# Attention with a hand-laid TensorE order: score matmuls spread over a head's slot, norm steps spread over slots

**The chip, the cores and the metric.** One core of a Trainium2 chip. The metric is device time in microseconds (us). Every kernel was run four to seven times, the kernel before again in each round; medians are quoted, with lowest and highest. Ratios are the mean time of one kernel's fast runs over the mean of the kernel before in the same rounds, so they are not quite the ratio of the quoted medians; in brackets stands the 95% interval. The experiments ran on two chips (6 and 9 to 12 on one, the others on another), so compare them by ratios. Every run here was of the fast state. A trace shows one run of each kernel; where that was not a typical one, the text says so.

## The reference

```python
def reference(A_x, A_k_cache, A_v_cache, A_wq, A_wo, B_x, B_w1, B_w2, B_w3, B_w4):
    x = A_x                                  # 1 x 2048 x 576
    xn = _layernorm(x, axis=-1)
    s = _A_ref(xn, ...)   # 32 heads of 128 dims over the last 512 keys of 16 kv heads, then @ wo
    g = _silu(_B_ref(xn, ...))
    # B: h = gelu(LN(xn) @ w1); four channel groups shifted along the sequence; x1 = xn + shifted @ w2
    #    out = x1 + gelu(LN(x1) @ w3) @ w4          (F = 4608)
    return x + s * g
```

## The kernel before

The sequence is cut into four blocks of 512 rows. Attention walks through 128 *slots*, one per head and block. A slot holds the next head's q (5 matmuls of 512 columns), this head's scores (4 of 512), the last head's value product (16 of 129), and now and then a *filler*: the output projection (wo) of the block before, W1 or W2. The MLP with w3 and w4 follows.

```python
        ps_sc = pool("ps_sc", 3, PSUM)       # score banks
        ps_pq = pool("ps_pq", 2, PSUM)       # q and W1
        ps_po = pool("ps_po", 2, PSUM)       # value product
        ps_wo = pool("ps_wo", 1, PSUM)
        ...                                  # cut
        def stage_s(u):
            ...
            for kc in range(KCH):            # four score matmuls, one after the other
                sc = ps_sc.tile([P, QB], FP32, name="sc", tag="sc")
                nc.tensor.matmul(sc[:, :], lhsT=kT[:, g, kc * P:(kc + 1) * P], rhs=qT[:, :], start=True, stop=True)
                pT = pT_pool.tile([P, QB], BF16, name="pT")
                nc.scalar.activation(out=pT[:, :], in_=sc[:, :], func=ACT.Exp, scale=SCALE)
        ...                                  # cut
            at(base + 8, lambda b=b: ln2(b))                    # norm before W1
            for tt in range(TB):
                at(base + 9, lambda b=b, tt=tt: tr2(b, tt))     # its transposes, sync engine's queue
        ...                                  # cut
        for j in range(2, NB * 8):
            at(4 * (j - 1), lambda j=j: load_wq(j))             # wq for four heads, two buffers
        ...                                  # cut
        with tc.manual_schedule(engines={SP, POOL}):            # TensorE is left to the scheduler
            for u in range(0, max(U + 2, last) + 1):
                if u + 1 < U:
                    stage_q(u + 1)
                if u < U:
                    stage_s(u)
                if 0 <= u - 1 < U:
                    stage_v(u - 1)
                if 0 <= u - 2 < U:
                    stage_t(u - 2)
                for fn in fill.get(u, []):
                    fn()
```

Loads of wq, v and x1 and the DMA transposes (o to oT per head, the normed block to xnnT for W1 and to xT for the next q, kT) all stand in the sync engine's queue, in the order of these slots. GpSimd's queue loads W1, W2, wo and x.

Names in the lines below: `sc` are scores, `pT` their exps, `po` the value product (`o` once it is scaled), `psq` is q before its copy to `qT`, `ph` and `psx` are the results of W1 and W2, `pswo` that of wo, `hs` is a part of W1's output that is copied with a shift for W2, and `x1` is W2's result, which is stored and loaded again for the MLP's norm. VectorE also takes maxima of wq and kT; a flag made of them tells whether the scores are small enough for an exp without a maximum taken off.

## Time and profile before

| | before |
|---|---|
| median of 4 runs (908.18 to 909.05) | 908.82 us |
| span in the profile, mean granted clock | 905.1 us, 0.988 |
| TensorE busy | 95% |
| bare slot, block 0 / blocks 1 to 3 | 3.06 / 3.10 us |
| slot with a W1 filler, blocks 1 to 3 | 4.17 us |
| slot with a wo filler | 10.00 us |
| time of one block (first exp to first exp of the next), blocks 0, 1, 2 | 111.8, 141.8, 142.3 us |

Slot times are distances between the first exps of successive heads. A *stop*, here and below, is the distance between the starts of two matmuls in a row less the columns of the first at 2.4 per ns, worked out from the trace. It is a little longer than the same wait in a list of waits, which counts from a modelled end. The lines behind this are in the prediction. The four timed runs of before are not the profiled one, which took 906.96 us.

### The profile page before, as it was taken

Reading aid. Unit: us, or ns where it says so; the run is one execution under the profiler, and the core shown is the slowest. Engines: PE = TensorE matmul, PEld = TensorE weight load, DVE = VectorE, ACT = ScalarE, POOL = GpSimd, SP = SyncE. Lnnn points to the kernel's source line nnn. Section 1 sums busy time; section 2 is a strip of 40 time slices with the busy share of each in tenths; the row PEclk is TensorE's granted clock in tenths of the full one; section 3 lists DMA queues with packets and bytes.
Section 4 is the critical chain, followed back from the end, with each engine's and each line's share of the span. In section 5 each row is a group of like instructions: output and inputs, shape, how many; then the busy total and the mean of one; then the engine's idle time right before and its main releaser. Section 6 shows DMA issues by size and latency. Waiting matters only on the chain.

```text
span 905.1 us, 15932 instructions
## 1 busy us (share of the span) xinstructions
PE 859.1 (95%) x6304; PEld 473.4 (52%) x6412; DVE 394.4 (44%) x1237; ACT 433.6 (48%) x814; POOL 36.9 (4%) x75
## 2 busy tenths in 40 slices
PE   5999799999999999999998998999999999999996
PEld 2655465555565465555564554554444444444454
DVE  7689653469882337652126644300026008005023
ACT  2666473277784366686345666122233223224510
POOL 1503000000000100000000000100000000000000
PEclk9999899999999999999999999999999999999998
DMA  5998931162543243362134245695005003101001
GB/s 125 183 211 191 212 95 48 30 149 62 112 101 81 34 112 88 91 121 62 39 84 104 56 114 111 169 342 138 1 7 154 1 1 132 30 1 53 1 14 43
DMA packets 165073, 83.73 MB, mean 93 GB/s; under 512 B 120064, under 2 KB 163328, under 8 KB 164992
## 3 DMA queue, kind: packets, MB, share of 16 engines
q1 hardware_dynamic: 158944, 71.57, 33.9%
q0 software_dynamic: 2640, 7.83, 3.8%
q10 hardware_dynamic: 3408, 3.25, 1.1%
q8 instruction: 52, 0.85, 0.4%
q14 instruction: 29, 0.24, 0.1%
HBM read 47.07 MB, written 9.44 MB: 62 GB/s over the span
## 4 chain that ended last, share of the span: by engine, by line


## 5 line engine op out<-in xcount | busy, mean ns | idle before, releaser
L306 ACT ACTIVATE pT<-sc 128x512 bf16<-128x512 f32 x512 | 266.0, 608 | 48.2 <-PE sc L304 48.1
L319 PEld LDWEIGHTS <-pT 128*128 128x128 bf16 x2048 | 141.4, 99 | 76.5 <-issue 16.5
L564 PE MATMUL ph<-xT_b,w_s 128*128 128x512 bf16 x701 | 171.0, 380 | 0.9
L319 PE MATMUL po<-v_sb,pT 128*128 128x129 bf16 x2048 | 164.2, 222 | 7.1 <-DVE o L323 7.0
L289 PE MATMUL psq<-xT_b,wq_b 128*128 128x512 bf16 x600 | 154.2, 384 | 8.1 <-DMA wq_b<-in_A_wq_dram 6.0
L304 PE MATMUL sc<-qT,kT 128*128 128x512 bf16 x512 | 154.9, 384 | 6.1
L567 ACT ACTIVATE h<-ph 128x512 bf16<-128x512 f32 x144 | 85.7, 596 | 155.5 <-PE ph L564 150.2
L573 PE MATMUL pm<-w_s,h 128*128 128x512 bf16 x523 | 143.4, 380 | 0.1
L322 DVE RECIPROCAL ri<-po 128x2 f32<-128x2 f32 x256 | 42.7, 167 | 184.3 <-PE po L319 182.9
L584 DVE TENSOR_TENSOR bs<-pm,x 128x512 f32<-128x512 f32 (+3 forms) x18 | 11.1, 633 | 251.5 <-PE pm L573 203.6
L347 PE MATMUL pswo<-wo_sb,oT 128*128 128x512 bf16 x497 | 111.3, 380 | 1.0 <-issue 0.2
L323 DVE TENSOR_TENSOR o<-po,ri 128x256 bf16<-128x256 f32 x256 | 108.0, 422 | 6.4 <-DVE ri L322 0.3
L564 PEld LDWEIGHTS <-w_s 128*128 128x128 bf16 x720 | 63.8, 98 | 73.4
L574 PE MATMUL pr<-w_s,h 128*128 128x64 bf16 x540 | 99.2, 193 | 0.8
L295 ACT ACTIVATE qT<-psq 128x512 bf16<-128x512 f32 x96 | 57.3, 597 | 80.4 <-PE psq L289 80.3
L289 PEld LDWEIGHTS <-wq_b 128*128 128x128 bf16 x640 | 59.4, 98 | 64.7 <-DMA wq_b<-in_A_wq_dram 6.9
L573 PEld LDWEIGHTS <-h 128*128 128x128 bf16 x540 | 52.6, 98 | 63.7 <-issue 0.6
L347 PEld LDWEIGHTS <-oT 128*128 128x128 bf16 x512 | 49.6, 98 | 57.0
L304 PEld LDWEIGHTS <-kT 128*128 128x128 bf16 x512 | 50.6, 99 | 45.9 <-issue 1.8
L350 ACT ACTIVATE s_out<-pswo 128x512 bf16<-128x512 f32 x16 | 9.6, 597 | 104.2 <-PE pswo L347 104.2
L574 PEld LDWEIGHTS <-h 128*128 128x128 bf16 x540 | 51.1, 98 | 12.2 <-issue 0.4
L586 ACT ACTIVATE th<-bs 128x576 f32<-128x576 f32 (+3 forms) x18 | 11.0, 626 | 44.5 <-DVE bs L584 44.5
(85 smaller groups left out, 455.7 us busy)
## 6 DMA issues: line engine op xcount, KB each, us to landing
wq_b<-in_A_wq_dram SPq DMA_DIRECT2D x32, 512.0 KB, 4.0
w_s<-in_B_w_dram SPq DMA_DIRECT2D x9, 576.0 KB, 8.1
wo_sb<-in_A_wo_dram POOLq DMA_DIRECT2D x4, 1152.0 KB, 7.7
w_s<-in_B_w_dram SPq DMA_DIRECT2D x9, 512.0 KB, 9.0
x_dram<-x SPq DMA_DIRECT2D x4, 576.0 KB, 3.5
x<-x_dram SPq DMA_DIRECT2D x4, 576.0 KB, 4.4
s_b<-s_dram SPq DMA_DIRECT2D x4, 576.0 KB, 6.0
x_b<-in_A_x_dram SPq DMA_DIRECT2D x4, 576.0 KB, 5.6
```

The costliest lines, as they stand in the source:

```text
L289: nc.tensor.matmul(psq[:, :], lhsT=w[:, kc, hh * Dh:(hh + 1) * Dh], rhs=xT_b[qb % 2][:, kc, :], start=(kc == 0), stop=(kc == NDC - 1))
L295: nc.scalar.activation(out=qT[:, :], in_=psq[:, :], func=ACT.Copy)
L304: nc.tensor.matmul(sc[:, :], lhsT=kT[:, g, kc * P:(kc + 1) * P], rhs=qT[:, :], start=True, stop=True)
L306: nc.scalar.activation(out=pT[:, :], in_=sc[:, :], func=ACT.Exp, scale=SCALE)
L319: nc.tensor.matmul(po[:, j, :], lhsT=pTs[kc][:, tt * P:(tt + 1) * P], rhs=v_sb[:, g, kc, 0:Dh + 1], start=(kc == 0), stop=(kc == KCH - 1))
L322: nc.vector.reciprocal(out=ri[:], in_=po[:, :, Dh])
L323: nc.vector.tensor_tensor(out=o[:, t0:t0 + 2, :], in0=po[:, :, 0:Dh], in1=ri[:].unsqueeze(2).to_broadcast([P, 2, Dh]), op=ALU.mult)
L347: nc.tensor.matmul(st["ps"][:, :], lhsT=oT_t[qb * Hq + h][:, tt, :], rhs=wo_sb[:, h, 0:M0], start=(h == 0), stop=(h == Hq - 1))
L564: nc.tensor.matmul(ph[:, :], lhsT=w3[:, kc, f0:f0 + P], rhs=xT_b[b % 2][:, kc, :], start=(kc == 0), stop=(kc == NDC - 1))
L567: nc.scalar.activation(out=h3[:, :], in_=ph[:, :], func=ACT.Gelu_apprx_tanh)
L573: nc.tensor.matmul(pm[tt][:, :], lhsT=lhsT, rhs=w4[:, fc % WS, 0:M0], start=(fc == 0), stop=(fc == FC - 1))
L574: nc.tensor.matmul(pr[:, tt, :], lhsT=lhsT, rhs=w4[:, fc % WS, M0:D], start=(fc == 0 and tt == 0), stop=(fc == FC - 1), skip_group_check=True)
```

## The change

Its intent: no burst of scores, hence no wait for a score bank; and no long run of norm operations on VectorE (DVE). The core of the diff:

```diff
-        with tc.manual_schedule(engines={SP, POOL}):
+        with tc.manual_schedule(engines={SP, POOL, PE}):
 ...
+                atoms = pe_fill.get(u, [])
+                cut = [atoms[0:n // 3], atoms[n // 3:2 * n // 3], atoms[2 * n // 3:]]
+                for i in range(4):
+                    if u < U:
+                        stage_s(u, i)
+                    if i == 0:
+                        if u + 1 < U:
+                            stage_q(u + 1)
+                        for fn in fill.get(u, []):
+                            fn()
+                        continue
+                    if i < 3 and 0 <= u - 1 < U:
+                        stage_v(u - 1, 2 * (i - 1))
+                    for fn in cut[i - 1]:
+                        fn()
 ...
-            at(base + 8, lambda b=b: ln2(b))
+            later(base + 7, lambda b=b: ln2_steps(b), 3)       # three steps of the norm a slot
-                at(base + 9, lambda b=b, tt=tt: tr2(b, tt))
+                at(base + 10, lambda b=b, tt=tt: tr2(b, tt))
-                at(base + 11 + c, lambda b=b, c=c: b1(b, c))
+                pe(base + 12 + c, b1(b, c))
-                o2 = base + (22 if bb == b else 16)
+                o2 = base + (24 if bb == b else 18)
```

Cut: the q copy and the eviction of the value product are marked high priority; an inverse root's Newton step uses three DVE operations in place of four; fillers are single matmuls; the other two norms move by a slot or more.

> **What bounds the kernel now.** I read the page's busy times and 40 slices first, then the list of waits, then the timeline of single head slots, the DMA queue's own timeline, and windows of a few microseconds. The page's chain that ended last is empty here, so the path is argued from TensorE (PE) itself.
>
> ```profile
> PE 859.1 (95%) x6304; PEld 473.4 (52%) x6412; DVE 394.4 (44%) x1237; ACT 433.6 (48%) x814; POOL 36.9 (4%) x75
> PE   5999799999999999999998998999999999999996
> PEclk9999899999999999999999999999999999999998
> ```
>
> PE looks busy in every slice, but a matmul's modelled end overlaps the next, so small gaps do not show; only start-to-start distances tell. Attention runs from 17 to 570 us (128 head slots, four blocks of 32), then the last output projection to about 601, then the MLP, whose diff is nil. One slot of block 1 with a filler (columns: start, length, engine, line, operation, count, idle before):
>
> ```profile
> 207.22 0.81 PE L304 MATMUL sc<-qT,kT 128*128 128x512 bf16 x3
> 207.42 0.60 ACT L295 ACTIVATE qT<-psq 128x512 bf16<-128x512 f32 x1 [1.11 <-PE psq L289]
> 207.87 0.63 PE L319 MATMUL po<-v_sb,pT 128*128 128x129 bf16 x8
> 207.91 1.08 ACT L306 ACTIVATE pT<-sc 128x512 bf16<-128x512 f32 x2
> 208.56 0.38 PE L304 MATMUL sc<-qT,kT 128*128 128x512 bf16 x1
> 208.56 0.66 PEld L319 LDWEIGHTS <-pT 128*128 128x128 bf16 x8 [0.18 <-issue]
> 208.77 0.63 PE L319 MATMUL po<-v_sb,pT 128*128 128x129 bf16 x8
> 209.24 1.24 PE L386 MATMUL ph<-xnnT,w_sb 128*128 128x512 bf16 x4
> 210.32 1.24 PE L289 MATMUL psq<-xT_b,wq_b 128*128 128x512 bf16 x5
> 211.39 0.81 PE L304 MATMUL sc<-qT,kT 128*128 128x512 bf16 x3
> ```
>
> The reader is to see the starts. Eight value matmuls take 0.47 us when nothing follows late (208.77 to 209.24), but 0.69 us before the fourth score matmul (207.87 to 208.56). That 0.22 us is the wait: there are three score banks, filled in one burst, and ScalarE (ACT), idle for 1.11 us before, first copies q and starts the first exp only at 207.91. The fourth score matmul waits until that exp ends. (At 209.24 there are five; one record is missing.) The slot lasts 4.17 us; without the wait, 3.95.
>
> The longer stops, from the list of waits (total us, times, longest) and the timeline:
>
> ```profile
> PE po L319 <- DVE o L323: 7.0, 2, 3.6
> PE psq L289 <- DMA wq_b<-in_A_wq_dram: 6.0, 3, 3.7
> PE ph L386 <- issue: 1.5, 2, 1.3
> PE ph L386 <- DMA xnnT<-xnn_b: 0.7, 2, 0.5
> ...
> 484.40 1.18 DVE L117 BATCH_NORM_STATS2 ln_st<-x 128x6 f32<-128x288 bf16 x3 [6.51 <-DMA x<-x_dram]
> ...
> 486.46 0.76 PE L319 MATMUL po<-v_sb,pT 128*128 128x129 bf16 x8 [3.33 <-DVE o L323]
> ...
> 480.00:500.00 20.00, 16.27 (x106) 8.91 (x106) 15.45 (x62) 10.45 (x21) 0.00 (x0) 0.91 0.35 88
> ```
>
> At 484 VectorE (DVE) sits in its queue on a norm's statistics whose input is still in flight, the value banks behind it are not emptied, and PE stops 3.33 us; afterwards the window's granted clock is 0.91 (the column before DMA share). I count four such stops: about 91 us (wq load, 3.67), 108 (wq load, 2.3), 483 (3.33) and 559 (3.64).
>
> **What the Trainium skill says.** "TensorE: Matmul & The Clock Gate", Back-to-back issue gap: a lone 512-column matmul is spaced N/2.4 + 2.5 ns, some 216 ns; the five q matmuls above take 1.07 us, so the trace agrees at 215. Its 81 ns for streamed 128-column matmuls with weight loads does not hold here: 0.47/8 is 58 ns. The same page, What's actually happening: an idle window of about 3.4 us halves PE's clock, for the next window. The trace agrees: 0.91 over 20 us is 3.4 us at half speed, 1.7 us lost. "ScalarE: Activation LUTs", What ACT_TABLE_LOAD costs: back-to-back activations overlap by about 93 ns. The trace agrees: one exp lasts 608 ns, yet four take 2.06 us at other places of the timeline, so a further one adds 0.515. ACT thus needs 4 x 0.515 + 0.5 for the q copy, about 2.6 us of a slot, and does not bound it. "Perfetto Trace Analysis", Optimization Strategy: consistent bubbles can mean too few buffers; the repeated 0.22 us is such a bubble, with three score banks, but the change cures it by order, not by banks.
>
> **The change part by part.** I compared the built orders of both kernels. PE has the same 13996 instructions; nothing is removed. Before, a slot is q5 s3 v8 s1 v8 plus filler. After, it is s1 q5 s1 v8 s1 v8 s1, with each filler cut in thirds after each v8 and after the last s. Fillers move by one or two slots. The ACT order becomes exp, q copy, exp, exp, exp. DVE loses three small operations in each norm (37 rows in all; 0.16 to 0.22 us each), off the path.
>
> *Slot length.* Bare PE time: 9 x 0.2155 for q and s, plus 2 x 0.466 for v: 2.87 us. Does ACT fit? An exp or copy starts 0.42 us after the start of the matmul that releases it (49.66 to 50.08, and 207.00 to 207.42). With the first s at 0, q's last matmul starts at 1.08, copy at 1.50, second s at 1.29, its exp at 2.01, third s at 1.98, exp 2.52, last s at 2.66, exp 3.04, next slot's s at 2.87. Each score bank is needed again three s later: the second exp ends at 2.62, before 2.87. So no wait, and the copy ends at 2.1, in time. A bare slot of block 0 now takes 3.06 us (copy on DVE), of blocks 1 to 3 3.10 (exps at 261.81 and 264.91). Gain 0.19 x 32 = 6.1 and 0.23 x 96 = 22.1 us, 28.2 in all; filler slots gain alike, by the 4.17 to 3.95 above.
>
> *What DVE takes back.* It is full where block 0's norms lie:
>
> ```profile
> 80.00:84.00 4.00, 3.95 (x32) 2.25 (x32) 4.00 (x16) 2.64 (x6) 0.00 (x0) 1.00 1.22 126
> 88.00:92.00 4.00, 3.19 (x28) 1.88 (x26) 4.00 (x17) 2.61 (x6) 0.85 (x2) 1.00 1.13 303
> ```
>
> DVE (third busy column) has 4.00 of 4.00. In the built order the norms' operations still stand in slots 17 to 27; the source spreads them, but the scheduler had already hoisted and spread them so, and they barely move. Shorter slots find DVE full: I take back ten slots' 0.19, 1.9 us. In block 1, with the maxima on DVE (54 of 60 us busy from 200 to 260), I take back a third of 7.4, 2.5. Net 23.8 us.
>
> *The stops.* At 91 us: the wq load was issued 87.85 and landed at 94.9 while transposes, w2 and x loads filled the queues. Those stand as before; gain 0. At 108: four xT transposes (5.2 us of issue) stood before the wq load; they move from slot 22 to 26, behind it. If gone, 2.3 + 1.7 of clock; I count two thirds, 2.6. At 483: the x1 load now stands behind four xnnT transposes (5.25 us) and the statistics only one slot later. Load issued about 6 us into slot 106, landing 4.8 later (479.62 to 484.40) makes 10.7; the first value bank is free at about 13.8 after six statistics; PE wants it at 2 x 2.87 + 3.95 + 1.5 = 11.2. Stop 2.6 in place of 3.3, with the half clock: gain 1. At 559: statistics move from inside slot 125's results to behind slot 127's; only the last head can wait, and the projection needs it 6.7 us after starting. From 3.6 and two half-clock windows (3.4) I keep 2 and 1.7: gain 3.3. Sum 6.9.
>
> *A loss.* xnnT's transposes start after the head of slot 9 is finished rather than slot 8 and are wanted in slot 12 at 1.98 us: 3 x 2.87 + 1.98 - 3.3 = 7.3 us. They need 1.24 + 5.24 + 2.7 landing, 9.2. In before there were 8.35 us (329.45 to 337.8) and a stop of up to 1.3. So another 1.0 in each of four blocks: -4.
>
> Sum: 23.8 + 6.9 - 4 = 26.7; 908.97 - 26.7 = 882.
>
> **Rivals.** *Loads and queues bound block 0*: DMA share 1.22 and 1.13 above, sync engine in transposes most of the time. For: the stop at 91 is this already. Against: only bursts exceed 1; 60 to 80 us has 0.75. Then block 0's 4 us come back as longer wq stops, and block 1's as late maxima: about 889 to 892. *In-order PE turns brittle*: every late exp, tanh or norm stops all work, because no scheduler put other matmuls in. For: ACT [...]holds tanh's of the filler among exps. Against: the old order was also fixed and had negative slack at one s a slot, the new has some 0.25 us bare and over 1 us in filler slots. If it holds, half of the 24 goes: about 894. *The stops vanish*: if the spread keeps every stop under the idle window, all four (13 us) and their half clocks (8.5) go, while xnnT still costs: about 868 to 870. Against: the order still shows statistics waiting for x1.
>
> **Range and chances.** Slots are the sure part; stops can move by 10 either way. I say 882, 870 to 895. Two per cent is 890.8: faster 0.8, within 0.18, slower 0.02.
>
> **What would show it.** Right: slots of 2.87 to 2.95 bare, 3.95 to 4.05 with a W1 filler, in blocks 2 and 3; no wait before the fourth s; a wq stop near slot 23 of block 0; a stop of 1 to 3 us at the first W1 matmul of each block; a stop in slot 108 or 109 on the results of DVE. Wrong: bare slots still 3.05 or more, ACT saturated, or the gain coming mainly from the vanished stops and a clock of 1.00 throughout.

## The result, and the profile after

| | before | after |
|---|---|---|
| median of 4 runs | 908.82 us | 892.91 us (891.93 to 893.64) |
| ratio, 95% interval | | 0.9825 (0.9808 to 0.9842) |
| span, mean clock | 905.1, 0.988 | 890.8, 0.988 |
| bare slot, block 0 / blocks 1 to 3 | 3.06 / 3.10 | 2.88 / 2.88 |
| slot with W1 / with wo | 4.17 / 10.00 | 3.96 / 9.78 |
| blocks 0, 1, 2 | 111.8, 141.8, 142.3 | 112.8, 139.2, 136.2 |
| slots 96 to 127 | 150.9 | 141.5 |
| from slot 127's first exp to the end | 340.7 | 343.9 |
| stops over 0.35 us from the first transposes to the first output group, sum | 19.1 | 28.8 |
| time at half clock until then | 17.1 | 17.1 |

The kernel is 1.75% faster: inside the predicted range, but short of the 2% to which the prediction gave 0.8. The page of the changed kernel, same lines as in the prediction:

```profile
PE   4979899999899999999998999899999999999996
PEclk9989999999999999999999999999999999999999
```

The first row dips in the third slice (a 7), where the row of before had a 9, and the clock row shows an 8 there: a stop in block 0 that was not there before. The slot itself did what was meant. A slot of block 2 with a W1 filler, from the timeline of the changed kernel (start, length, engine, line, operation, count, idle before):

```profile
344.56 1.24 PE L303 MATMUL psq<-xT_b,wq_b 128*128 128x512 bf16 x5
345.64 0.38 PE L318 MATMUL sc<-qT,kT 128*128 128x512 bf16 x1
...
345.86 0.63 PE L335 MATMUL po<-v_sb,pT 128*128 128x129 bf16 x8
...
346.33 0.38 PE L407 MATMUL ph<-xnnT,w_sb 128*128 128x512 bf16 x1
...
346.54 0.38 PE L318 MATMUL sc<-qT,kT 128*128 128x512 bf16 x1
...
346.76 0.63 PE L335 MATMUL po<-v_sb,pT 128*128 128x129 bf16 x8
...
347.65 0.38 PE L318 MATMUL sc<-qT,kT 128*128 128x512 bf16 x1
...
348.30 0.38 PE L318 MATMUL sc<-qT,kT 128*128 128x512 bf16 x1
...
348.52 1.24 PE L303 MATMUL psq<-xT_b,wq_b 128*128 128x512 bf16 x5
```

Both runs of eight value matmuls take 0.47 us to the next start (345.86 to 346.33, and 346.76 to 347.22 where the filler resumes), and no score matmul waits. From q to q it is 3.96 us. The list of waits of the changed kernel (total, times, longest) shows what stands against this:

```profile
PE ph L407 <- DMA xnnT<-xnn_b: 9.9, 4, 6.0
PE psq L303 <- DMA wq_b<-in_A_wq_dram: 4.8, 6, 2.1
PE pswo L359 <- DMA oT<-o: 2.6, 1, 2.6
PE psx L450 <- DVE hs L439: 2.3, 1, 2.3
PE po L335 <- DVE o L340: 2.3, 1, 2.3
```

W1's wait for xnnT was 0.7 us in before, or 2.0 with the 1.3 that the list of before puts under "issue" (it ended at 339.33, just after the last transpose had landed, at 339.24); it is 9.9 now, and 6.0 of it is one stop. Compare the queues around it. Before, the queues of the sync engine and of GpSimd:

```profile
45.34 5.20 SPq L255 DMA_TRANSPOSE xnnT<-xnn_b  x4
...
51.28 0.88 POOL L227 DMA_DIRECT2D wo_sb<-in_A_wo_dram  x1 [0.29 <-issue]
```

After, with the matmul that waited:

```profile
49.83 7.23 SPq L269 DMA_TRANSPOSE xnnT<-xnn_b  x4
...
49.98 0.89 POOL L242 DMA_DIRECT2D wo_sb<-in_A_wo_dram  x1 [0.29 <-issue]
...
59.57 0.58 PE L407 MATMUL ph<-xnnT,w_sb 128*128 128x512 bf16 x1 [6.03 <-DMA xnnT<-xnn_b]
```

Before, the four transposes were through before the 1152 KB load of a quarter of wo began. Now both start within 0.15 us, the transposes hold the sync queue for 7.23 us in place of 5.20, and they take longer to land. The view of the tile xnnT in block 0, before and after (from the issue of one to its landing):

```profile
DMA to landing us min/median/max: 2.7/3.2/4.1
DMA to landing us min/median/max: 5.6/6.1/7.3
```

TensorE stops 6.2 us between starts. The clock is granted by half from 57.26 to 64.09, 6.8 us; TensorE stands still in the first 2.3 of them, and the matmuls of the rest take 2.2 us longer than at full clock.

### The profile page after: what moved, and what is told of

Its sections match the earlier page's. It is cut to its first block, busy times and chain, and to the rows that moved or that the text cites. A ratio compares the mean times of both kernels' runs of the same rounds, so it can differ in the third digit from the quotient of the medians.

```text
span 890.8 us, 16129 instructions
## 1 busy us (share of the span) xinstructions
PE 847.1 (95%) x6412; PEld 468.0 (53%) x6412; DVE 387.6 (44%) x1201; ACT 456.1 (51%) x814; POOL 36.7 (4%) x75
## 4 chain that ended last, share of the span: by engine, by line
## 5 line engine op out<-in xcount | busy, mean ns | idle before, releaser
L320 ACT ACTIVATE pT<-sc 128x512 bf16<-128x512 f32 x512 | 290.5, 596 | 120.0 <-PE sc L318 112.0
L318 PE MATMUL sc<-qT,kT 128*128 128x512 bf16 x512 | 184.1, 382 | 1.7 <-DVE qT L308 1.5
L303 PE MATMUL psq<-xT_b,wq_b 128*128 128x512 bf16 x640 | 160.6, 382 | 4.8 <-DMA wq_b<-in_A_wq_dram 4.8
L643 PE MATMUL pm<-w_s,h 128*128 128x512 bf16 x540 | 145.8, 380 | 0.0
L359 PE MATMUL pswo<-wo_sb,oT 128*128 128x512 bf16 x512 | 118.2, 382 | 2.6 <-DMA oT<-o 2.6
L303 PEld LDWEIGHTS <-wq_b 128*128 128x128 bf16 x640 | 62.4, 98 | 82.7 <-DMA wq_b<-in_A_wq_dram 7.7
L359 PEld LDWEIGHTS <-oT 128*128 128x128 bf16 x1024 | 65.3, 98 | 59.1 <-DMA oT<-o 3.1
L318 PEld LDWEIGHTS <-kT 128*128 128x128 bf16 x512 | 47.6, 98 | 32.9 <-issue 3.7
L407 PE MATMUL ph<-xnnT,w_sb 128*128 128x512 bf16 x100 | 33.2, 398 | 10.9 <-DMA xnnT<-xnn_b 9.9
```

The lines of the kernel that those rows point to most:

```text
L303: nc.tensor.matmul(psq[:, :], lhsT=w[:, kc, hh * Dh:(hh + 1) * Dh], rhs=xT_b[qb % 2][:, kc, :], start=(kc == 0), stop=(kc == NDC - 1))
L359: nc.tensor.matmul(ps, lhsT=oT_t[qb * Hq + h][:, tt, :], rhs=wo_sb[:, h, lo:hi], start=(h == 0), stop=(h == Hq - 1))
L643: nc.tensor.matmul(pm[tt][:, :], lhsT=lhsT, rhs=w4[:, fc % WS, 0:M0], start=(fc == 0), stop=(fc == FC - 1))
```

## The experiments

All gave the right result, and none was refused. My theory at the start: the order inside the slot gives the gain, and late xnnT transposes take a third of it back (A). The rivals: the norm steps matter; the queues are short whatever one does. Each experiment is an edit of the kernel after unless it says otherwise. The diffs are cut to the lines that matter.

**1. xnnT two slots earlier.**

```diff
-            later(base + 7, lambda b=b: ln2_steps(b), 3)
+            later(base + 5, lambda b=b: ln2_steps(b), 3)
-                at(base + 10, lambda b=b, tt=tt: tr2(b, tt))
+                at(base + 8, lambda b=b, tt=tt: tr2(b, tt))
```

> The changed kernel with one edit: each block's second norm and its four xnnT transposes stand two slots earlier in the sync engine's queue (slots 5 to 8 in place of 7 to 10); TensorE's order is the same, instruction by instruction. Theory A (the change itself made these stops, by cutting the lead of the transposes over the first W1 matmul): the waits of W1 matmuls for xnnT (9.9 us in the changed kernel, 6.0 in block 0) go to under 1 us, the half-speed window after the one in block 0 goes too, and the time falls from 893 by 9 to 14 us, to 879 to 884. Theory B (block 0 is bound by queues and loads as a whole): the same time comes back as longer waits for wq or K in block 0, and the time stays above 888.

Measured: 896.26 us (893.04 to 900.37), ratio 0.9879 (0.9829 to 0.9928). Theory A fell on the time and B held (over 888, with longer waits for wq), although the W1 waits went as A said. From its trace, the list of waits and the lines around 46 to 56 us:

```profile
PE psq L303 <- DMA wq_b<-in_A_wq_dram: 18.8, 8, 5.3
```

```profile
46.29 5.18 SPq L269 DMA_TRANSPOSE xnnT<-xnn_b  x4
...
51.57 0.54 SPq L206 DMA_DIRECT2D wq_b<-in_A_wq_dram  x1
...
55.28 1.89 PE L303 MATMUL psq<-xT_b,wq_b 128*128 128x512 bf16 x4 [5.34 <-DMA wq_b<-in_A_wq_dram]
```

W1 no longer waits, but q does: 18.8 us against 4.8. The transposes now stand ahead of slot 8's wq load, which is issued at 51.57 right behind them and beside the same wo load (51.46). The place in the sync queue had only been given to another customer. This held in every block (q stops of 3.2, 2.3 and 2.5 us in blocks 1 to 3), so it is not block 0's traffic alone. The total is not clearly worse than after's (0.9825, 0.9808 to 0.9842): the intervals overlap.

**2. The old order inside the slot, pinned.** TensorE stays under manual order, but q 5, s 3, v 8, s 1, v 8, then the filler. (The conditions on u are left out.)

```diff
-                for i in range(4):
-                    ...
+                stage_q(u + 1)
+                stage_s(u, 0)
+                for fn in fill.get(u, []): fn()
+                stage_s(u, 1); stage_s(u, 2)
+                stage_v(u - 1, 0)
+                stage_s(u, 3)
+                stage_v(u - 1, 2)
+                for fn in atoms: fn()
```

> The changed kernel with TensorE's old order inside each slot, pinned by hand (five q, three scores, eight values, one score, eight values, then the filler whole); slots of the fillers, norms, priorities as in the changed kernel. Theory A (the gain is the fourth score matmul's wait): bare slots of blocks 1 to 3 go back from 2.88 to 3.10 us, W1 slots from 3.96 to 4.17; 128 slots times 0.2 is +26, less about 4 where longer slots give the transposes more lead: 910 to 918. Rival (the gain comes from norms, priorities or moved fillers): 890 to 897.

Measured: 904.01 us (901.84 to 908.26), ratio 0.9968 (0.9921 to 1.0015), under the expected range. In blocks 1 to 3 the slots are 3.10, 4.17 and 10.0 us again: the score wait, undone and back. But block 0's bare slot is 2.88 and not 3.06. The timelines tell why. Before, block 0:

```profile
44.20 0.40 PE L319 MATMUL po<-v_sb,pT 128*128 128x129 bf16 x4
...
44.61 0.38 PE L304 MATMUL sc<-qT,kT 128*128 128x512 bf16 x1
```

This experiment, block 0:

```profile
42.66 0.63 PE L335 MATMUL po<-v_sb,pT 128*128 128x129 bf16 x8
43.13 0.38 PE L318 MATMUL sc<-qT,kT 128*128 128x512 bf16 x1
```

The scheduler had put the fourth score after four value matmuls, whose 0.23 us had become 0.41 by the wait; after eight there is none (0.47). In block 0 DVE copies q and not ScalarE (ACT). There the first exp ends 1.01 us after the start of the first score, and the fourth score, after eight, comes at 1.12; in blocks 1 to 3 that exp ends at 1.28, and the fourth score has to wait until 1.34. So pinning alone cures block 0; the even spread is needed in blocks 1 to 3. This kernel kept the high priorities, the moved fillers and the spread norms, and it is not shown to be faster than the kernel before: its interval holds 1.

**3. Norms whole, old Newton, all else as after.**

```diff
-                at(u + i // per, step)
+                at(u + 1, step)
```

> The changed kernel with each norm put in one slot as a whole and with the old, longer Newton step, all else as in the changed kernel. Theory A (the spreading is without effect, since the scheduler places VectorE's operations by itself, and VectorE is off the path but for the few stops): 893 plus or minus 2. Rival (spreading keeps the values' results from waiting behind a norm): 898 or more, with more waits of value matmuls for VectorE.

Measured: 891.72 us (891.57 to 897.96), ratio 0.9849 (after: 0.9825). No difference that these runs show (the interval is 0.98 to 0.9898, three runs of four took 891.6 to 891.8): spreading the norms is worth nothing that can be measured. The Newton lines of the edit are not printed.

**4. The kernel before with spread norms and the short Newton alone**, TensorE left to the scheduler.

```diff
-            at(base + 8, lambda b=b: ln2(b))
+            later(base + 6, lambda b=b: ln2_steps(b), 3)
-                at(base + 21, lambda b=b: ln1(b + 1))
+                later(base + 19, lambda b=b: ln1_steps(b + 1), 3)
```

> The kernel before with the norms split into steps over three slots and the shorter Newton step, transposes in their old slots, TensorE left to the scheduler. Theory A: 909 plus or minus 3, the bare slot still 3.10 us, the four long stops still there. Rival (the spread norms are what helps): 900 or less.

Measured: 905.23 us (904.0 to 906.13), ratio 0.9974 (0.9938 to 1.0009): 0.8 us under theory A's range, and not shown to differ from the kernel before. Its slots are 3.06 and 3.10 us, its long stops those of before. With experiments 2 and 3: the order on TensorE is what the change is worth.

**5. xnnT two slots and wq one slot earlier.** Since 1 had only swapped the customers, this one serves both. The wq buffer is free by then, except that block 1's maxima read it, so they move a slot too. (A third wq buffer would be the plainer test; it was not run.)

```diff
-            at(4 * (j - 1), lambda j=j: load_wq(j))
+            at(4 * (j - 1) - 1, lambda j=j: load_wq(j))
-                at(Hq + 4 * j + (kc + 1) // 2, lambda j=j, kc=kc: wq_max(j, kc))
+                at(Hq + 4 * j - 1 + (kc + 1) // 2, lambda j=j, kc=kc: wq_max(j, kc))
```

> The changed kernel with xnnT's four transposes issued two slots earlier (as in the first experiment) and, new, every wq load issued one slot earlier, so that the load stands ahead of those transposes in the sync engine's queue (its maxima move one slot too, to free the buffer). Theory A, the sync engine's queue is served in order and only the place in it counts: both the stop before the first W1 matmul of a block (6.0, 1.5, 2.0, 0.9 us in the changed kernel) and the wq stops that replaced it in the first experiment (5.5, 3.2, 2.3, 2.5) go to under 1 us each, and two half-clock windows with them: 893 less some 10 for xnnT, 3 for the wq stops at 98 and 125 us, and 3.4 of clock, so 876 to 882. Theory B, the 16 DMA engines are short in block 0 and loads land late wherever they stand: blocks 1 to 3 gain their 4.4, block 0 keeps 5 us of stops: 887 to 890. Theory C, the maxima hold the buffer and the queue stops behind the load: over 893.

Measured: 880.81 us (878.27 to 881.86), ratio 0.9702 (0.9664 to 0.974): theory A. No wait for xnnT is left in its list, and q's wait is

```profile
PE psq L303 <- DMA wq_b<-in_A_wq_dram: 2.3, 2, 1.2
```

Block 0 fell from 112.8 to 104.3 us, block 2 from 136.2 to 133.7.

**6. wq one slot earlier alone.** The first edit of 5 without that of 1.

> The changed kernel with the wq loads one slot earlier and xnnT's transposes where the change put them: the other half of the experiment that gave 881. Theory A (place in the sync queue): the wq stops at 98, 125, 265 and 401 us go (2.2 + 1.0 + 0.95 + 0.74 + 0.4 and one half-clock window of 1.7), the xnnT stops (6.0, 1.5, 2.0, 0.9 us) stay: 893 less 6, so 885 to 889, and the rest of the way to 881 belongs to xnnT. Theory B (the two only help together, since each wins what the other has lost): 891 to 895.

Measured: 888.09 us (883.89 to 890.07), ratio 0.9784: theory A, with xnnT's stops as in after (6.25, 1.64, 1.76, 0.90). Neither edit 0.9825, xnnT alone 0.9879, wq alone 0.9784 (0.9752 to 0.9817), both 0.9702: the same move of xnnT gains 0.8% with wq ahead, and does not gain with wq late (there the ratio is 0.5% higher, with overlapping intervals). The waits in the traces say why: what counts is the order in the queue.

**7. wq loads from GpSimd's queue, xnnT two slots earlier.** The transposes themselves were not moved to a second queue: the Trainium skill, "DMA: Bandwidth & Descriptors", Silent corruption: two transposing streams in flight at once, says that two streams that transpose at the same time can corrupt each other's result. No run here shows that; I kept away from it.

```diff
-            nc.sync.dma_start(out=w[:, 0:NF, :],
+            nc.gpsimd.dma_start(out=w[:, 0:NF, :],
```

> The changed kernel with xnnT's transposes two slots earlier and the wq loads issued from GpSimd's queue in place of the sync engine's, at the same slots as before. Theory A (order in the sync queue): a load is then never behind transposes; the wq stops and the xnnT stops both go, 876 to 882, as with the load one slot earlier. Theory B (DMA engines or the landing itself): the wq load still lands late in block 0 (stops of 2 to 5 us near 50 and 98), 887 to 896. If the load of GpSimd stands behind its own gates for W1, W2 and wo, a stop may show near slots 5, 11, 17 and 23 instead.

Measured: 895.04 us (890.35 to 900.31), ratio 0.9856 (0.9821 to 0.9891). The traced run was the slowest of five, 900.31 us. In blocks 1 to 3 it is as good as 5 (138.3, 133.7, 142.5 us against 137.9, 133.7, 141.7). Block 0 takes 120.2 us against 104.3. From its timeline:

```profile
36.15 0.86 POOL L206 DMA_DIRECT2D wq_b<-in_A_wq_dram  x1
...
41.09 1.04 PE L303 MATMUL psq<-xT_b,wq_b 128*128 128x512 bf16 x4 [2.06 <-DMA wq_b<-in_A_wq_dram]
```

The load stands behind the sixteen issues of W1, which GpSimd works through from 25.73 to 36.15; later a q stop of 6.3 us comes behind those of W2. GpSimd's queue has an order too. Theory A holds where that queue is empty and fails where it is not, as the last sentence of the expectation allowed.

**8. Two DVE stops.**

```diff
-        at(3 * Hq + 10, lambda: load_x1(0))
+        at(3 * Hq + 5, lambda: load_x1(0))
-            at(Hq + 2 * g + 1, lambda g=g: k_max(g))
+            at(2 * Hq + 2 * g + 1, lambda g=g: k_max(g))
-        at(2 * Hq + 4, finish_flag)
+        at(3 * Hq + 4, finish_flag)
```

> The changed kernel with two DVE stops treated: x1 is loaded five slots earlier in block 3, and the maxima of kT go from block 1 to block 2 (the flag one block later). Theory A, each stop is what its releaser says: the stop on DVE o at 477 us (2.44 and 0.95, with a half-clock window of 1.7) and the one on hs at 224 (2.47) go to under 0.5 us, total 885 to 888. Theory B, DVE is full anyway and its queue gives the stop elsewhere, or in block 2: 891 to 893.

Measured: 889.86 us (885.4 to 891.4), ratio 0.9799 (0.9752 to 0.9846), between the theories, and not clear of after's 0.9825; the stops are what can be read. The stop on hs fell from 2.47 to 0.68 us (DVE was full with maxima). The flag, one block later, made a stop of 1.55 of its own. At 472 us a stop of 2.25 remained, with another releaser, in DVE's timeline:

```profile
469.43 0.43 DVE L128 TENSOR_SCALAR xnn_b<-x,ln_mv,nr_y 128x576 bf16<-128x576 bf16 x1 [1.12 <-DMA xnnT<-xnn_b]
```

With x1 there earlier, the scheduler put the norm's last step further ahead too, and each of its four operations (469.43 to 473.75) waits in DVE's queue for the buffer that xnnT's transposes are still reading. Here an operation whose input came earlier was scheduled earlier, and then waited for the next thing.

**9. The old slot order in the kernel of 5**: what is the order worth with most queue stops gone?

> The 881 us version (xnnT two slots, wq one slot earlier) with TensorE pinned to the old order inside a slot (q 5, s 3, v 8, s 1, v 8, filler). With the long stops out of the way the price of the order should show bare. Theory A, the order is worth its 0.22 us a slot in blocks 1 to 3 and nothing in block 0 (where pinning alone gave 2.88 us): 0.22 x 96 = 21 more, 899 to 904. Theory B, the order is worth only the 11 us seen when the old order was put into the changed kernel, since faster slots meet queues sooner: 890 to 894.

Measured: 894.94 us (893.15 to 897.06), ratio 0.9862 against 0.9702: 1.6%, some 14.5 us, just above the range of B. Block 2, which has no stop in either kernel, takes 140.7 us against 133.7: 7.0 us in 32 slots, 0.22 each. Blocks 1 and 3 show 3.7 each in place of 7, and the tail is 3.2 us better with the old order (stop for oT 1.65 us against 2.81, and no half-clock window). Block 0 differs by 5.2 us although its slots are equal; that is stops, and not the order's worth (the traced run, 897.06 us, was the slowest of four). So A is right on the slot and wrong on the sum: the faster slot meets DVE and the last transposes sooner.

**10. One transfer moved.** Only the second quarter of wo starts in slot 14 in place of 11; the order on every engine stays.

```diff
-            at(5 + 6 * i, lambda i=i: late(pT_t[5 + 6 * i][0][0:1, 0:1], lambda: load_wo(i)))
+            at((5, 14, 17, 23)[i], lambda i=i: late(pT_t[(5, 14, 17, 23)[i]][0][0:1, 0:1], lambda: load_wo(i)))
```

> The changed kernel with one transfer moved: the second quarter of wo (1152 KB, from GpSimd's queue) is started in slot 14 of block 0 in place of slot 11. Every engine's order stays the same. In the changed kernel that load was issued at 49.98 us, beside the first of xnnT's transposes (49.83), which then took 7.23 us in the sync queue; in the kernel before the transposes (45.34 to 50.54) came ahead of it (51.28). Theory A, block 0's stop of 6.0 us is this collision on the DMA engines, on top of the 1 to 2 us by which the transposes start too late in every block: the stop falls to 1 to 2.5 us and the two half-clock windows at 57 us go (3.4 us), so 893 less 7 to 8: 884 to 887. Theory B, the stop is the late start and the transposes' own time: it stays over 4.5 us, 891 to 894.

Measured: 887.95 us (886.82 to 890.77), ratio 0.9799 (0.9772 to 0.9825). From its timeline:

```profile
48.73 5.18 SPq L269 DMA_TRANSPOSE xnnT<-xnn_b  x4
...
55.32 0.38 PE L407 MATMUL ph<-xnnT,w_sb 128*128 128x512 bf16 x1 [2.29 <-DMA xnnT<-xnn_b]
```

The transposes take 5.18 us again in place of 7.23, the stop 2.3 in place of 6.0, and both half-clock windows at 57 us are gone; block 0 takes 105.9 us in place of 112.8. The landing, which was 5.6/6.1/7.3 us:

```profile
DMA to landing us min/median/max: 2.6/2.6/3.3
```

So theory A is shown for the stop. The whole time came out 1 us above its range (5 us less than after by the medians, 0.3% by the ratios, with overlapping intervals): other stops grew (1.8 us on DVE at 78, and a half-clock window at 193). Of the 4.2 us by which the last transpose landed earlier, 1.1 is an earlier start (48.73 against 49.83), which came before the load in either trace. The other traces agree on the rest. In the eight kernels whose last transpose was issued at least 1.0 us before this load of wo, it landed 2.63 to 2.68 us after its issue; in the other six, issued at most 0.2 us before it or after it, 4.4 to 7.8.

**11. All together**: 5, plus x1 five slots earlier into a buffer that is free when the norm's turn comes, W2 a slot later, and the matmul that needs the last head's oT moved from the end of the last projection's first group into its second.

```diff
-    xm_b = [xnn_b, xn_b[0]]
+    xm_b = [xn_b[0], xnn_b]
-                o2 = base + (24 if bb == b else 18)
+                o2 = base + (24 if bb == b else 19)
+        tail = wo_atoms(NB - 1)
+        tail[1] = tail[1][:24] + tail[0][-1:] + tail[1][24:]
+        tail[0] = tail[0][:-1]
```

> The 881 us version with the three remaining named stops treated: the first MLP block's norm writes another buffer (free when its turn comes) and its x1 is loaded five slots earlier (stop of 4.25 us at 460 us plus a half-clock window of 1.7); W2 one slot later (stop of 2.0 at 215 on the shifted copy hs); and in the last output projection the matmul that needs the last head's oT moves from the end of the first group into the second (stop of 2.8 at 544, and its half clock of 1.7). Theory A, each stop is its own: 12 us in all, less what DVE gives back, so 868 to 873. Theory B, DVE's order puts the wait elsewhere (as in the experiment that only moved the load): 877 to 881.

Measured: 874.25 us (872.66 to 876.46), ratio 0.9637 (0.9616 to 0.9657). That is just above theory A's range, and well under B's. The stops at 460 and 544 us are gone, and with them 5.9 us of slots 96 to 127 and 4.5 of the tail. Block 0 took 6.0 back (the traced run, 876.46 us, was the slowest of five): xnnT landed late again, beside the wo load issued at 51.6 us, and TensorE stopped 4.2 us.

In the kernel of 5 the four were issued from 45.20 to 50.39, the last landed at 51.79, and the load began at 51.37. Here they started 2.3 us later, the last one was issued at 51.41, 0.17 before the load, and it landed at 59.20.

**12. The same with the wo quarter moved.**

> The version of all treatments (874 us, in which block 0 still stopped 4.24 us for xnnT) with the same quarter of wo moved to slot 14. Theory A (collision on the DMA engines): that stop and its half-clock window (1.7) go, 867 to 870. Theory B (the stop comes from the queue or from the norm's own lateness): 873 to 876. If the moved load collides with the wq load of slot 15, a wq stop near slot 19 takes part of it back: 870 to 873.

Measured: 873.72 us (872.59 to 879.48), ratio 0.9635: no gain; the time is in theory B's range, though the xnnT stop is gone as A says. In the trace block 0 still takes 110.4 us, with stops of 1.1 to 2.3 us on DVE and on wq in its place; but this was the slowest of seven runs, 5.8 us over the median. What bounds block 0 then is not settled; one more move of one load did not help. Version 11, or this one, beats the kernel after by 1.9% and the kernel before by 3.6% (by ratios).

## Why the prediction was partly right

The steps in order, with the gain predicted and what the two traces show (us; positive is gained). What half clock costs is counted from the trace: by how much the matmuls in such a window are longer than at full clock, 1.3 to 1.7 us in a window of 3.4, and 2.2 to 2.3 in the two of 6.8, because TensorE stands still in a part of them.

| step of the prediction | predicted | measured |
|---|---|---|
| slot length, 28.2 | 28.2 | 0.18 x 32 + 0.22 x 95 = 26.7 |
| DVE takes back | -4.4 | -3: hs in block 1 (waits of 2.3 against 0.3), and W1 slots up to 4.3 |
| stops for wq (91 and 108 us) | 2.6 | stops 6.5 to 5.8, clock 3.1 to 1.4: 2.4 |
| stop at 483 | 1 | 3.5 + 0.6 to 2.4 + 0.95, clock 1.3 to 1.5: 0.5 |
| stop at 559 | 3.3 | 3.8 + 1.0 to 2.7 + 0.5, clock 2.3 to 1.5: 2.3 |
| loss by xnnT | -4 | block 0: -5.8 and -2.2 of clock; blocks 1 to 3: -2.2; in all -10.2 |
| start of attention | none | -1.9 (first scores wait for DVE's q copy) |
| sum | 26.7 | 16.8 (medians: 15.9; these two traces: 14.3) |

So 2.5 us of what the traces lost are in none of these steps; 0.5 of that is a longer MLP, the rest is not explained.

*The slot was right*, to 0.01 us: 2.88 bare against a predicted 2.87, 3.96 against 3.95 with W1, no wait for an exp before the fourth score, and experiments 2 and 9 put the old order back and get the 0.22 us back. Its explanation was complete for blocks 1 to 3 only. For block 0 the scheduler's place for the fourth score was the cause, and pinning it was enough.

*The term that was mis-sized* is the loss: "So another 1.0 in each of four blocks: -4." For blocks 1 to 3 it measured 2.2 against 3. In block 0 it cost 8.0 with the half clock, where 1 was foreseen. The step took the transposes' 5.24 us and their landing from other blocks and asked only when they start; that a 1152 KB load starts in the same slot 11 stood in the kernel's text, at the place from which wo is loaded. Experiment 10 shows the collision: one load moved by three slots, with no engine's order changed, takes 3.7 us off the stop (up to 1.1 of them by an earlier start), and both windows of half clock go.

*Two readings in the prediction were off, without touching its sum.* The 2.7 us for the landing count from an issue's start (188.93 to 191.60 in before), but were added to its end: the need is some 7.9 us and not 9.2. And the trace does not agree with the page's overlap of 93 ns: four exps in 2.06 us, the last of them 0.61 long, start 0.48 us apart, so a further one adds 0.48 and not 0.515, and the overlap is 0.12 us. ACT needs 2.4 us of a slot and not 2.6.

*The rivals.* "Loads and queues bound block 0" named the right place and nearly the right time (889 to 892); it expected the time back as longer wq stops, where it came as an xnnT stop. The two are the same resource: experiments 1 and 5 show that one becomes the other. The brittle order did not show in stops from late exps or tanh's: none is in the list over 0.5 us. The third rival, all stops gone, was wrong; their sum rose from 19.1 to 28.8. As announced, there was a wq stop near slot 23 (2.2 us), one at the first W1 matmul of each block (6.2, 1.5, 2.0 and 0.9 us, where 1 to 3 were announced), one in slot 109 on DVE.

*The chances.* The 0.8 for over 2% hung on slots as the sure part, and they were. But 2% is 18 us, and any 9 us of new stops spend that margin. A range of 25 us and four unsized collisions did not support 0.8.

*Left open*: what bounds block 0 once xnnT, wq and wo are placed (experiment 12), and why the transposes started 2.3 us later in the kernel of 11 than in that of 5, whose orders there were meant alike.

## What to carry to other kernels

When TensorE's slot gets shorter, every transfer that was just in time comes too late: before counting the gain, list for each queue what stands in it around each deadline, and what other load starts then. Moving one transfer earlier moves the wait to the one behind it; move the whole train, or none. And moving work inside an in-order queue only helps if what it waits for next is also free.

## What the Trainium skill lacked or had wrong

- "TensorE: Matmul & The Clock Gate", Back-to-back issue gap: 81 ns for sustained 128-column matmuls with weight loads. Eight of 129 columns took 0.47 us, 58 to 59 ns each, in both kernels. The 131 ns that stand beside it for 512 columns do not hold either: five took 1.07 us, about 215 ns each.
- The same page, What's actually happening: half clock after an idle window of about 3.4 us. In before a stop of 2.3 us (108 us) and in after one of 2.7 (556 us) were each followed by a 3.4 us window at half clock, while stops of 2.5 (224 us) and 2.0 (336 us) were not; a whole idle window is not needed.
- "DMA: Bandwidth & Descriptors": for a transpose within SBUF it has sequencer cycles of "previous generations", in a table about another chip and without the transfer; I found nothing on what another load does to one. Four of 128 x 640 took 5.2 us of the sync queue and the last landed 2.6 to 2.7 us after its issue; beside a load of 1152 KB they took up to 7.2, and the last landed after 4.4 to 7.8.
